# Splitting one pair of weight transfers into pieces of 15, 24 and 25 partitions

## The chip, the core and the metric

The kernel runs on one core of one Trainium2 chip. A core has a matrix engine (TensorE, PE in the profile), three engines for elementwise work (VectorE or DVE, ScalarE or ACT, GpSimd or POOL), a synchronising engine (SyncE, SP) and 16 DMA engines, which move data between the chip's main memory and the on-chip memory of 128 partitions. The metric is the time of one execution in microseconds (us), taken on the device; lower is better.

## What is computed

Linear attention with a feature map, then a layer that mixes channels for 64 Fourier modes along the sequence, then a residual with a rectified product. In the reference's own terms, cut short:

```python
# q, k, v: 8 batches x 8 heads x 576 x 64; phi(x) = exp(+-(x @ w_phi)), scaled
kv = einsum('bhsf,bhsd->bhfd', phi(k), v);  z = sum(phi(k), axis=2)
x  = (phi(q) @ kv) / (phi(q) @ z + 1e-6)            # to 8 x 576 x 512
X  = rfft(x, axis=1)[:, :64]                        # 64 modes
Yr = einsum('bmd,mde->bme', Xr, w_r) - einsum('bmd,mde->bme', Xi, w_i)
Yi = einsum('bmd,mde->bme', Xr, w_i) + einsum('bmd,mde->bme', Xi, w_r)
u  = x + irfft(Y, n=576)
out = u + maximum(u @ w_ch, 0)
```

`w_r` and `w_i` hold 64 matrices of 512 x 512 in 32-bit floats, 67 MB each. They are by far the largest inputs, and every element is used once per execution.

## The kernel before

**Stages.** The first stage walks over 32 steps of attention (two heads of one batch, or one head of two batches, in each) and computes feature maps, attention, and the forward Fourier transform of the result into `XT`. The mode products run beside it, as soon as the heads that they need are done. When the attention is finished, a loop over the remaining groups of modes goes on until all are summed (lines 852 to 903), and a last stage of 18 units makes the output: products with the inverse transform and with `w_ch`, a rectifier, sums, and stores (lines 905 to 927).

**Groups of weights.** The weights come in 32 groups, numbered k = 0 to 31 (lines 108 and 109). Group k has a pair (g, gi): a block of input channels and a set of modes. From k = 8 on, a group is 8 modes x 128 channels, for the real and for the imaginary weights: two tiles `wr` and `wi` of 128 partitions x 8 x 512. The 28th group is k = 27, with g = 3 and gi = 3. Its products (`mode_mm`, line 438) accumulate in PSUM over the real tile first and the imaginary tile second, and `mode_sum` adds them to what earlier groups left in `Yacc`.

**How a group is loaded.** `weights(k)` (line 156) makes a list of four issues: real weights for partitions 0 to 63 (y = 0), real for 64 to 127 (y = 1), then imaginary for the two halves. Each is one DMA from GpSimd's queue (line 169) with 64 partitions x 4 modes x 1024 elements, which reads 32-bit floats and writes bfloat16: 512 KB written. Within a partition, a run of 1024 elements is contiguous on both sides. In the last loop, `modes_of(k, 0)` (line 834) issues the groups up to k + 2 before it computes group k, so k = 27 is issued in the turn of k = 25. The tiles `wr` and `wi` have three buffers each (line 45), so a group may be loaded when the products of the group three before it are done.

**What orders the work.** The program's order is written out by hand (`manual_schedule`, lines 561 and 849); each engine runs its instructions in that order and waits on semaphores. The transfers from GpSimd's queue share eight semaphores in rotation: a transfer waits until the one eight places before it has landed, so at most eight are in flight. TensorE's first product of a tile waits for the transfers of that tile. In the last loop a turn holds, on TensorE, the real products of the group, a product with `w_ch` (`psW`, line 700), a transposition (`pt`, line 689), the imaginary products, the transposition of the sum (`ptY`, line 831), and every second turn a regrouping by batch (`psZY`, lines 726 and 732).

Of the kernel before, what the change touches and what calls it, by code (L numbers as in the profile page):

```python
# [26 lines left out]
def kernel(  # L27
# [11 lines left out]
    nc = tc.nc  # L39
# [116 lines left out]
    def weights(k):  # L156
        g, gi = groups[k]
        W[k] = wt = {}
        for ri, w in ((0, moe_w_r), (1, moe_w_i)):
            for y in range(2):  # L160
                def issue(ri=ri, w=w, y=y):
                    if y == 0 and k == 0:
                        wt[ri] = Yacc.rearrange("p a e -> p (a e)").bitcast(BF16).rearrange(
                            "p (r m e) -> p r m e", r=2, m=8)[:, ri]
                    elif y == 0:
                        wt[ri] = pw.tile([128, 8, DMODEL], BF16, name=f"w{'ri'[ri]}", tag=f"w{ri}")
                    t = wt[ri][64 * y:64 * y + 64]
                    if gi >= 0:
                        nc.gpsimd.dma_start(  # L169
                            t.rearrange("p (m i) e -> p m (i e)", i=2),  # L170
                            w[8 * gi + y:8 * gi + 8:2, g * 128:(g + 1) * 128, :].rearrange(
                                "m (p i) e -> p m (i e)", i=2))
                    else:
                        m0 = 16 * (-1 - gi) + 8 * y
                        nc.gpsimd.dma_start(
                            t, w[m0:m0 + 8, g * 64:(g + 1) * 64, :].rearrange("m p e -> p m e"))
                due.append((k, issue))
# [383 lines left out]
    with tc.manual_schedule():  # L561
# [22 lines left out]
        for n in range(N + 2):  # L584
# [54 lines left out]
            e = n - (N + 2 - N_EARLY)  # L639
# [209 lines left out]
    with tc.manual_schedule():  # L849
        flip_x()  # L850
        flip_x()
        for k in range(k_out, 31):
            gi = groups[k][1]
# [36 lines left out]
        rows = slice(96, 128)  # L890
# [14 lines left out]
        at_end, t, free = [], 0, 0  # L905
# [52 lines left out]
```

## Time and profile before

| what | value |
|---|---|
| median of 3 runs | 447.03 us (446.74 to 447.61) |
| the profiled execution's own time | 446.91 us |
| its span in the profile | 445.1 us |
| TensorE busy, of the span | 312.2 us (70%) |
| VectorE busy | 292.9 us (66%) |
| ScalarE busy | 271.7 us (61%) |
| GpSimd busy | 217.6 us (49%) |
| weights, real: transfers from line 169 and line 175, median time from issue to landing | 62 of 512 KB, 18.7 us |
| weights, imaginary | 62 of 512 KB, 18.6 us |

No computing engine is busy over 70% of the span, while in all but the last slices of the profile's overview the 16 DMA engines are busy 90% or more. A DMA engine's work is listed by queue: q0 holds the transfers that GpSimd issues, q1 those of SyncE and ScalarE, and q8 the blocks of instructions that an engine fetches as it goes through its program. The overview gives a mean over the 16 DMA engines; where they differ from each other has to be read from the end of a stage, where some run out of work before others.

### The profile page before, as it was taken

How to read it: one execution, taken by the hardware profiler on the slowest of the kernel's cores; microseconds unless marked ns; L12 is line 12 of the kernel's file. 1: busy time of each engine (PE TensorE's matmuls, PEld its weight loads, DVE VectorE, ACT ScalarE, POOL GpSimd, SP SyncE). 2: the span in 40 equal slices, each digit the busy share in tenths (PEclk: the TensorE clock that was granted, in tenths of full speed). 3: DMA queues.
4: the chain of work that ended last, by engine and by line, in shares of the span. 5: the costliest groups of instructions: out<-in, count | busy, mean ns of one | idle time of the engine just before them, and what ended most of it. 6: DMA issues, size and time to landing. Idle time of an engine off the chain costs nothing.

```text
span 445.1 us, 11874 instructions
## 1 busy us (share of the span) xinstructions
PE 312.2 (70%) x4997; PEld 202.9 (46%) x4997; DVE 292.9 (66%) x420; ACT 271.7 (61%) x570; POOL 217.6 (49%) x301
## 2 busy tenths in 40 slices
PE   1668587675966776765464667776898768777992
PEld 0456465564655654554342544433444434433440
DVE  4788889889788688878643886653232445264782
ACT  3766787886786886786652866662254445354761
POOL 6776448585457566556542654441142222100891
PEclk9999999989596599799966998887699898999997
DMA  8999999999999999999999999999999999991797
GB/s 191 248 225 218 221 226 219 230 219 218 229 222 222 223 231 221 225 231 222 231 212 222 222 222 211 211 211 211 211 206 212 210 211 211 210 201 32 253 354 278
DMA packets 60885, 97.76 MB, mean 220 GB/s; under 512 B 3888, under 2 KB 28784, under 8 KB 60832
## 3 DMA queue, kind: packets, MB, share of 16 engines
q0 software_dynamic: 51888, 76.69, 95.7%
q1 hardware_dynamic: 8784, 20.26, 13.2%
q8 instruction: 39, 0.64, 0.5%
q10 hardware_dynamic: 160, 0.07, 0.1%
q14 instruction: 14, 0.11, 0.1%
HBM read 163.64 MB, written 9.44 MB: 389 GB/s over the span
## 4 chain that ended last, share of the span: by engine, by line
DMA 38%; PE 24%; DVE 22%; ACT 8%; issue 4%; POOL 3%; DVEq 0%; SPq 0%; ACTq 0%; POOLq 0%
DMA wi<-in_moe_w_i_dram 22%; DVE mkq L248 8%; DMA k<-in_k_dram 8%; DMA wr<-in_moe_w_r_dram 5%; DVE nd L337 3%; DVE xs_all L351 3%; PE psY L438 3%; PE psWe L409 2%; ACT AA L255 2%; ACT AA L259 2%; PE psB L772 2%; PE ptr L199 2%; PE psB L779 2%; PE psA L793 2%; DMA kn<-in_k_dram 2%
## 5 line engine op out<-in xcount | busy, mean ns | idle before, releaser
L285 POOL TENSOR_TENSOR vaug<-vn,ee 128x576 bf16<-128x576 f32 x64 | 73.2, 1164 | 50.3 <-ACT ee L270 46.5
L255 ACT ACTIVATE AA<-psT 128x1024 bf16<-128x1024 f32 x64 | 62.0, 1021 | 23.9 <-PE psT L223 23.2
L169 POOL DMA_DIRECT2D wr<-in_moe_w_r_dram x48 | 29.7, 619 | 73.5 <-PE psY L438 24.8
L277 ACT ACTIVATE e<-mkq 64x4 f32<-64x4 f32 (+1 forms) x128 | 26.3, 206 | 58.8 <-DVE mkq L248 56.4
L259 ACT ACTIVATE AA<-psk 128x1024 bf16<-128x1024 f32 x64 | 61.3, 1008 | 0.0
L169 POOL DMA_DIRECT2D wi<-in_moe_w_i_dram x48 | 29.9, 625 | 44.8 <-DMA wi<-in_moe_w_i_dram 17.2
L248 DVE TENSOR_REDUCE mkq<-psq 128x8 f32<-128x1024 f32 x32 | 38.9, 1217 | 0.6 <-PE psq L214 0.4
L248 DVE TENSOR_REDUCE mkq<-psk 128x8 f32<-128x1024 f32 x32 | 38.7, 1210 | 0.7 <-PE psk L214 0.7
L438 PE MATMUL psY<-wi,XT 128*32 128x512 bf16 x192 | 17.7, 442 | 27.2 <-DMA wi<-in_moe_w_i_dram 27.2
L438 PEld LDWEIGHTS <-XT 128*32 128x32 bf16 x384 | 14.9, 172 | 45.6 <-DMA wi<-in_moe_w_i_dram 20.6
L702 ACT CAST xw<-psW 128x512 bf16<-128x512 f32 x34 | 19.9, 585 | 25.5 <-PE psW L700 25.0
L700 PE MATMUL psW<-wchb,sT 128*128 128x512 bf16 x136 | 34.0, 395 | 0.0
L692 DVE COPY sT<-pt 128x1024 bf16<-128x1024 bf16 x17 | 11.8, 692 | 33.7 <-PE pt L689 33.7
L330 DVE TENSOR_TENSOR tB<-psNB,e 128x650 f32<-128x650 f32 x32 | 26.6, 831 | 9.5 <-PE psNB L320 9.0
L205 DVE COPY kT<-ptr 128x640 bf16<-128x640 bf16 x32 | 15.7, 491 | 25.7 <-PE ptr L199 25.7
L320 PEld LDWEIGHTS <-AA 128*128 128x128 bf16 x640 | 28.4, 109 | 8.2 <-issue 7.8
L199 PE MATMUL ptr<-ident_b,k 128*128 128x128 bf16 x160 | 17.9, 257 | 19.4 <-DVE qT L205 15.9
L223 PE MATMUL psT<-qT,w 64*128 64x512 bf16 x64 | 15.2, 463 | 22.4 <-DVE mkq L248 22.2
L301 PE MATMUL kvz<-vaug,AA 64*128 64x65 bf16 x1152 | 28.5, 208 | 2.1 <-DVE Yacc L453 1.3
L351 DVE TENSOR_TENSOR xs_all<-nd,rden 128x640 bf16<-128x640 f32 x32 | 28.5, 892 | 1.1
L337 DVE TENSOR_TENSOR nd<-psNA,tB 128x650 f32<-128x650 f32 x32 | 26.7, 835 | 3.7 <-DVE tB L330 0.5
L301 PEld LDWEIGHTS <-AA 64*128 64x128 bf16 x1152 | 24.2, 105 | 6.4 <-issue 2.1
(141 smaller groups left out, 732.0 us busy)
## 6 DMA issues: line engine op xcount, KB each, us to landing
wr<-in_moe_w_r_dram POOLq DMA_DIRECT2D x62, 512.0 KB, 18.7
wi<-in_moe_w_i_dram POOLq DMA_DIRECT2D x62, 512.0 KB, 18.6
out_dram<-of SPq DMA_DIRECT2D x14, 512.0 KB, 3.9
vn<-in_v_dram SPq DMA_DIRECT2D x24, 288.0 KB, 6.0
q<-in_q_dram POOLq DMA_DIRECT2D x12, 288.0 KB, 16.7
k<-in_k_dram POOLq DMA_DIRECT2D x12, 288.0 KB, 16.8
vn<-in_v_dram SPq DMA_DIRECT2D x16, 144.0 KB, 6.7
Yacc<-in_moe_w_r_dram POOLq DMA_DIRECT2D x2, 512.0 KB, 8.8
```

What stands on the lines that cost most here:

```text
L169: nc.gpsimd.dma_start(t.rearrange("p (m i) e -> p m (i e)", i=2), w[8 * gi + y:8 * gi + 8:2, g * 128:(g + 1) * 128, :].rearrange("m (p i) ...
L199: nc.tensor.transpose(ptr[:, c, :], tb[:, 2 * c:2 * c + 2, :].rearrange("p j d -> p (j d)"), ident_b,)
L248: nc.vector.tensor_reduce(out=o, in_=i, axis=AX.X, op=ALU.max, apply_absolute_value=True)
L255: nc.scalar.activation(AA[:, 0, ab, 0:1024].rearrange("f (x j p) -> f j x p", j=2, p=64), st["psT"].rearrange("f j (x p) -> f j x p", p=64 ...
L259: nc.scalar.activation(AA[:, 1, ab, 0:1024].rearrange("p (c j f) -> p j c f", c=4, j=2), st["psk"], ACT.Exp, scale=sc)
L285: nc.gpsimd.tensor_tensor(out=vaug[:, ab, :, 0:64], in0=st["v"], in1=ee[:, ab, :].unsqueeze(2).to_broadcast([128, 9, D_]), op=ALU.mult,)
L301: nc.tensor.matmul(kvz[:, hh, ab * 65:(ab + 1) * 65], lhsT=AA[r, 1, ab, 128 * j:128 * j + 128], rhs=vaug[r, ab, j, :], start=(j == 0), sto ...
L320: nc.tensor.matmul(p[:, hh, 65 * c:65 * c + 65], lhsT=AA[:, 0, ab, x:x + 128], rhs=kvzF[:, hh, ab * 65:(ab + 1) * 65], start=True, stop=True,)
L337: nc.vector.tensor_tensor(out=nd, in0=st["psNA"], in1=st["tB"], op=ALU.add)
L351: nc.vector.tensor_tensor(out=xo, in0=nd[:, :, :, 0:64], in1=rden.to_broadcast([128, 2, NCH, 64]), op=ALU.mult,)
L438: nc.tensor.matmul(psY[32 * j:32 * j + 32, :], lhsT=XT[:, 16 + 32 * ri:48 + 32 * ri, 32 * i + 4 * gi + j], rhs=wt[ri][:, 2 * j + i, :], st ...
L700: nc.tensor.matmul(ps, lhsT=sT[:, x, dc, :], rhs=wchb[:, dc, :], start=(dc == 0), stop=(dc == 3))
```

## The change

For group k = 27, and there for the real weights alone, each of the two transfers of 64 partitions is issued as three: partitions 0 to 14, 15 to 38 and 39 to 63 of the half, that is 15, 24 and 25 partitions. The bytes, the source rows and the destination are the same. All other groups, and the imaginary weights of this one, keep their transfers of 64 partitions.

```diff
                     if gi >= 0:
-                        nc.gpsimd.dma_start(
-                            t.rearrange("p (m i) e -> p m (i e)", i=2),
-                            w[8 * gi + y:8 * gi + 8:2, g * 128:(g + 1) * 128, :].rearrange(
-                                "m (p i) e -> p m (i e)", i=2))
+                        dst = t.rearrange("p (m i) e -> p m (i e)", i=2)
+                        rows = w[8 * gi + y:8 * gi + 8:2, g * 128:(g + 1) * 128, :].rearrange(
+                            "m (p i) e -> p m (i e)", i=2)
+                        cuts = (0, 15, 39, 64) if k == 27 and ri == 0 else (0, 64)
+                        for p0, p1 in zip(cuts, cuts[1:]):
+                            nc.gpsimd.dma_start(dst[p0:p1], rows[p0:p1])
```

## The prediction

> **What bounds the kernel now.** I read the chain of waits first, cut to the time after 305 us. Columns: start in us, length in us, what the end waited for.
>
> ```profile
> 325.73 0.60 POOL wi L169
> 326.33 18.80 DMA wi<-in_moe_w_i_dram
> ...
> 345.41 19.72 DMA wi<-in_moe_w_i_dram
> ...
> 365.41 19.60 DMA wi<-in_moe_w_i_dram
> ...
> 385.30 19.60 DMA wi<-in_moe_w_i_dram
> 404.90 0.04 issue
> 404.94 0.69 PE psY L438 x8
> 405.63 0.54 PE psA L787 x2
> ```
>
> From 326 to 404.9 us the end waits for nothing but weight transfers. What follows the last landing, up to the end of the run, is a chain of its own: 446.91 - 404.90 = 42.0 us (446.91 is the profiled execution, with a span of 445.1). A change before 405 us counts as far as it moves the last landing.
>
> Next, GpSimd's queue in order of time (start, length, instruction, idle time before it and its releaser), around group 27, which the diff splits: the two wr rows are what it replaces.
>
> ```profile
> 338.20 0.61 POOL L169 DMA_DIRECT2D wr<-in_moe_w_r_dram  x1 [2.13 <-DMA wr<-in_moe_w_r_dram]
> 340.44 0.61 POOL L169 DMA_DIRECT2D wr<-in_moe_w_r_dram  x1 [1.62 <-DMA wr<-in_moe_w_r_dram]
> 343.22 0.61 POOL L169 DMA_DIRECT2D wi<-in_moe_w_i_dram  x1 [2.18 <-PE psW L700]
> 345.41 0.61 POOL L169 DMA_DIRECT2D wi<-in_moe_w_i_dram  x1 [1.57 <-DMA wi<-in_moe_w_i_dram]
> ```
>
> An issue takes 0.61 us, then GpSimd idles 1.6 to 2.2 us until an older transfer has landed. In the built program each transfer waits for the semaphore of the eighth transfer before it, so eight are in flight. Later rows of the view have the first wi of a group at 343.22 and at 383.06 us, four groups or 16 transfers apart: 39.84 / 16 = **2.49 us per transfer**. That agrees with 512 KB at 211 GB/s (2.485 us), so the transfers run back to back.
>
> Third, busy time in short stretches up to the last landing. The last two columns are the mean busy share of the 16 DMA engines (about 1.12 when all are busy, since packets overlap) and GB/s.
>
> ```profile
> 398.00:399.00 1.00, 0.76 (x10) 0.64 (x10) 0.30 (x2) 0.12 (x1) 0.00 (x0) 1.00 1.14 215
> 399.00:400.00 1.00, 1.00 (x7) 0.41 (x5) 0.57 (x1) 0.26 (x1) 0.00 (x0) 1.00 0.79 147
> 400.50:401.00 0.50, 0.50 (x9) 0.27 (x8) 0.00 (x0) 0.39 (x1) 0.00 (x0) 1.00 0.64 119
> 402.50:403.00 0.50, 0.50 (x4) 0.22 (x3) 0.00 (x0) 0.28 (x1) 0.00 (x0) 1.00 0.56 106
> 403.50:404.00 0.50, 0.00 (x0) 0.00 (x0) 0.00 (x0) 0.14 (x1) 0.00 (x0) 1.00 0.31 57
> 404.00:404.50 0.50, 0.00 (x0) 0.00 (x0) 0.00 (x0) 0.00 (x0) 0.00 (x0) 1.00 0.18 33
> ```
>
> The engines do not finish together. Soon after 399 us about half have run out of work (0.64 / 1.12 = 57% are left at 400.5 us, 50% at 402.5), and the rest need until 403 to 404.5 us. The trace's landing signs say the same: a transfer gives sixteen, and those of the last one come in two groups of eight, from 399.43 to 401.48 and from 403.58 to 404.90 us. This spread of 5.4 us is the same for every transfer after 330 us, so both groups run at one pace and one is behind. The queue rows suggest what put it behind:
>
> ```profile
> q0 software_dynamic: 51888, 76.69, 95.7%
> q8 instruction: 39, 0.64, 0.5%
> ```
>
> Blocks of instructions used 0.5% of 16 x 445.1 us = 35.6 us of DMA engine time, 39 packets of 0.91 us. In the packet records their lengths repeat every eight packets, as if eight engines took them in turn: 35.6 / 8 = 4.5 us each, about the gap between the groups. So the late eight would be those that also fetch instructions. Full levelling could win: engine time left after 399.0 us, over all stretches, is 3.02 us by shares, / 1.12 = 2.70, so a level end at 401.7 in place of 404.5 us, **2.8 us at most**.
>
> **The change, part by part.**
>
> *Bytes and their shares.* Nothing is removed: 128 partitions of group 27's real weights move as before, in runs of the same length. A transfer of 64 partitions gives an engine 64 / 16 = 4, so one partition costs 2.49 / 4 = **0.62 us** on its engine, and an engine that gets p of the 128 in place of 8 moves by (p - 8) x 0.62. All later transfers have even shares, so a shift stays to the last landing. No row shows how 15, 24 or 25 partitions are dealt. The bounds are -2.8 us (levelled) and, if a piece of 25 stays with a single engine in both halves, (50 - 8) x 0.62 = +26 us; with 64 or 128 partitions, the only transfers of weights, q and k here, the shares are equal. I stay by these rows: equal shares on as many engines as divide the piece, the next piece going on where the last one stopped. That is 15 engines with 1, 12 with 2, 5 with 5: 32 runs, twice round the ring, so the second half repeats the first. Per half, 11 engines get 1 + 2 = 3, four get 1 + 5 = 6, one gets 2 + 5 = 7 (33 + 24 + 7 = 64). Over both halves eleven have 6 in place of 8 (-1.24 us), four 12 (+2.49), one 14 (+3.73). The Trainium skill, DMA: Bandwidth & Descriptors, section "Why a DMA increments its semaphore by 16 and not by 1", states such a rule: the largest count up to 16 that divides the slowest dimension, on consecutive engines from a round-robin cursor; no run here shows it yet, and its exception is the first rival.
>
> *On whom the surplus falls.* No row numbers the engines. I assume that both the pieces and the instruction blocks are dealt from the first engine on: then the surplus falls on the last five and the late group is the first eight. The late eight move by -1.24; the surplus engines, of the early group, end at most at 401.48 + 2.49 = 403.97 or near 399.5 + 3.73 = 403.2, against 404.90 - 1.24 = 403.66. So the gain is 0.93 to 1.24 us; I take 1.24, as only one of the early eight is as late as 401.48.
>
> *Four more transfers.* Each engine posts four more landing signs; the packet records show 22 ns for one: +0.09 us. By the Trainium skill, same page, "Anatomy of one DMA", a transfer from GpSimd costs some 2.0 us beside its bytes, which would make +8 us if it were paid in turn. The pace of 2.49 us is bytes alone, so here it is hidden.
>
> *GpSimd's queue.* Four more issues, 4 x 0.61 = 2.44 us, lie in its idle time. But the pieces take six places of the eight in flight: they are issued one per landing, from 338.2 to about 350.5 us, and group 27's two wi behind them at 352.9 and 355.4 in place of 343.2 and 345.4. The cover shrinks by four transfers, from 19.6 us to about 10. The late engines begin the pieces at 355.1 us and have 6 x 0.62 + 2.49 = 6.2 us of work before they need the second wi, issued at 355.4; a 64 KB transfer from GpSimd lands 2.0 us after issue (list of DMA issues), so 4.2 us of cover are left: cost 0. Without this cover it would be up to the 2.0 us. The early engines, 5.4 us ahead, may idle 1 to 1.5 us there, which costs nothing while they stay 4 us ahead. Next are group 28's transfers, which wait for the pieces' semaphores and so go out within 3 us of each other.
>
> *TensorE.* Its first wr product of group 27 waits for six semaphores in place of two; behind it stand psW, pt and the wi products. The last piece lands near 359 us, before TensorE gets there at 360.7, so no cost. TensorE must take up the earlier landings (timeline of PE):
>
> ```profile
> 365.17 0.69 PE L438 MATMUL psY<-wi,XT 128*32 128x512 bf16 x8 [1.53 <-DMA wi<-in_moe_w_i_dram]
> ...
> 404.94 0.69 PE L438 MATMUL psY<-wi,XT 128*32 128x512 bf16 x8 [1.49 <-DMA wi<-in_moe_w_i_dram]
> ```
>
> It is idle 1.53 and 1.49 us ahead of them, more than is won, so the gain passes through; 1.49 is its ceiling.
>
> **Sum:** -1.24 + 0.09 = -1.15; 446.91 - 1.15 = **445.8 us**. The median of the runs shown is 447.03, 0.12 above the profiled one; the same step from it gives 445.9.
>
> **Rivals.**
> 1. *Slower: dealt by rounding up from the first engine.* 15 as 1 on 15 engines, 24 as 2 on 12, 25 as 2 on 12 and 1 on one: twelve engines get 5 of 64, the others 3, 1, 1, 0. At most four engines are relieved and at least four late ones get 10 in place of 8. It decides as soon as one of those near 404.9 is among the twelve: +1.24 + 0.09 = +1.33, 448.2 us. For it: nothing in the rows but that it also gives 4 each for 64. The Trainium skill, in the section named first, reports as an exception that some copies from GpSimd were dealt so (100 partitions on engines 0 to 14); no run here shows it.
> 2. *Slower: equal runs, but the surplus meets late engines.* A late engine with 12 in place of 8 ends 2.49 later: +2.58, 449.5 us; with 14, up to +3.8, 450.7. For it: half of all engines are late. Against: they look like one block of eight. The Trainium skill, same page, "Latency and other measured facts", calls engines 7 and 15 usually the slow ones, and engine 15 would have the 14; this trace shows eight late ones, not two.
> 3. *The shares stay even.* Then only +0.09, 447.0 us.
>
> **Chances.** Forecast 0.56, first rival 0.18, second 0.14, third 0.12. A measurement of this kernel tells about 0.2% (0.9 us) from no change, so faster 0.56, same 0.12, slower 0.32. The likeliest case alone is 445.4 (TensorE's ceiling) to 446.1 (gain of 0.84). The range goes from 445.2 (the ceiling, and the runs' own scatter of some 0.3 us below their median) to 448.6, over the first rival; the second is left out, and with it the +26 us of a piece on one engine, which no row comes near.
>
> **What would show it.** Right: the last landing near 403.7 us; the late half's stretch shorter by 1.2 us with the early half's end spread to 402 to 403; GpSimd's six issues some 2.5 us apart; TensorE idle only 0.3 us ahead of the last wi products; 42.0 us after the landing unchanged. Rival 1: two groups still, the last landing near 406.2. Rival 2: one to five engines alone at 407 or later. Wrong altogether: a stretch after 350 us in which the late engines idle, or an issue of a piece that takes several us.

## The result, and the profile after

The change made the kernel slower: median 450.09 us (449.5 to 450.88, 4 runs) against 446.88 us before, ratio 1.007 with a 95% interval of 1.0058 to 1.0083, some 3.2 us. The forecast was 445.8 us, and its range ended at 448.6; the second rival (equal runs, surplus on late engines) had 449.5. The profiled execution took 449.50 us with a span of 447.7 us.

The chain of waits of the changed kernel, cut to its last part (start, length, what the end waited for):

```profile
355.67 12.27 DMA wi<-in_moe_w_i_dram
...
368.23 19.59 DMA wi<-in_moe_w_i_dram
...
388.10 19.58 DMA wi<-in_moe_w_i_dram
407.68 0.04 issue
407.72 0.67 PE psY L440 x7
```

It is still weight transfers to the last landing, at 407.68 us in place of 404.90: **+2.78 us**. What follows is 449.50 - 407.68 = 41.8 us long, 42.0 before. So all of the loss lies ahead of the last landing. (Of the 3.2 us between the medians, the profiled pair shows 2.6; the changed kernel's profiled execution was its fastest.)

GpSimd's queue around group 27 (start, length, instruction, idle time before it and its releaser):

```profile
338.44 0.60 POOL L174 DMA_DIRECT2D wr<-in_moe_w_r_dram  x1 [2.22 <-PE ptY L833]
340.58 0.60 POOL L174 DMA_DIRECT2D wr<-in_moe_w_r_dram  x1 [1.54 <-DMA wr<-in_moe_w_r_dram]
343.07 0.68 POOL L174 DMA_DIRECT2D wr<-in_moe_w_r_dram  x1 [1.89 <-DMA wi<-in_moe_w_i_dram]
345.54 0.54 POOL L174 DMA_DIRECT2D wr<-in_moe_w_r_dram  x1 [1.80 <-DMA wi<-in_moe_w_i_dram]
348.06 0.57 POOL L174 DMA_DIRECT2D wr<-in_moe_w_r_dram  x1 [1.97 <-DMA wr<-in_moe_w_r_dram]
350.52 0.68 POOL L174 DMA_DIRECT2D wr<-in_moe_w_r_dram  x1 [1.88 <-DMA wr<-in_moe_w_r_dram]
353.75 0.64 POOL L174 DMA_DIRECT2D wi<-in_moe_w_i_dram  x1 [2.55 <-PE psY L440]
355.67 0.62 POOL L174 DMA_DIRECT2D wi<-in_moe_w_i_dram  x1 [1.29 <-DMA wi<-in_moe_w_i_dram]
356.77 0.61 POOL L174 DMA_DIRECT2D wr<-in_moe_w_r_dram  x1 [0.47 <-DMA wr<-in_moe_w_r_dram]
```

The six pieces go out one per landing, 2.1 to 2.5 us apart, the two wi behind them at 353.8 and 355.7 us, and then group 28 quickly. The issue times are within a microsecond of those worked out. No issue takes longer than 0.68 us.

Busy time by stretch (the last two columns are the mean busy share of the DMA engines, 1.12 when all are busy, and GB/s), first around the pieces, then up to the last landing:

```profile
345.00:350.00 5.00, 3.38 (x44) 1.72 (x48) 1.11 (x2) 0.00 (x0) 1.12 (x2) 0.65 1.12 210
350.00:355.00 5.00, 4.95 (x60) 2.20 (x54) 2.43 (x2) 2.59 (x3) 1.32 (x2) 0.67 1.00 177
...
401.00:402.00 1.00, 0.48 (x6) 0.36 (x7) 0.42 (x1) 0.00 (x0) 0.00 (x0) 1.00 0.71 131
403.00:404.00 1.00, 1.00 (x5) 0.39 (x4) 0.25 (x1) 0.57 (x1) 0.00 (x0) 1.00 0.40 76
405.00:406.00 1.00, 1.00 (x6) 0.49 (x5) 0.00 (x0) 0.12 (x1) 0.00 (x0) 1.00 0.29 55
406.00:407.00 1.00, 1.00 (x6) 0.29 (x3) 0.00 (x0) 0.72 (x2) 0.00 (x0) 1.00 0.22 41
407.00:408.00 1.00, 0.42 (x6) 0.37 (x8) 0.00 (x0) 0.33 (x1) 0.00 (x0) 1.00 0.04 6
```

Two things are new. From 350 to 355 us the engines move 177 GB/s in place of 210, at a busy share of 1.00 in place of 1.12: some of them stand still for a part of the time. And the end has a third step: from 405 to 407 us the share is 0.29 to 0.22, that is 0.29 / 1.12 x 16 = 4.1 engines. **Four engines run on alone.** The trace's sixteen landing signs of the last transfer, one for each DMA engine, in us, show the same (the bar stands where the wide gap is):

```
before: 399.43 399.47 399.51 399.51 399.71 399.91 400.51 401.48 | 403.58 403.59 403.60 404.05 404.17 404.78 404.85 404.90
after:  401.38 401.39 401.44 401.48 401.58 401.62 401.92 402.19 402.34 403.26 404.11 404.31 | 406.61 407.34 407.44 407.68
```

TensorE in order of time, at group 27's two products:

```profile
363.64 0.68 PE L440 MATMUL psY<-wr,XT 128*32 128x512 bf16 x8 [1.68 <-DMA wr<-in_moe_w_r_dram]
...
367.99 0.67 PE L440 MATMUL psY<-wi,XT 128*32 128x512 bf16 x8 [1.39 <-DMA wi<-in_moe_w_i_dram]
```

The wr product now waits 1.68 us for the pieces, where it had been covered; the last piece landed at 363.5 us, not near 359.

Not all of the 2.78 us comes from the pieces. The landing that frees GpSimd at 335 us, before any piece is issued, is at 335.18 us before and at 335.32 with the change. From there to the last landing it is 69.72 us before and 72.36 with the change: **+2.64 us**. The landing at 335 us is used as a common start below, too; it holds to 0.1 or 0.2 us, as the engine that is last there need not be the last at the end.

### The profile page after: what moved, and what is told of

Same layout as the page of the kernel before. It is cut to its first block, busy times and chain, and to the rows that moved or that the text cites. A ratio compares the mean times of both kernels' runs of the same rounds, so it can differ in the third digit from the quotient of the medians.

```text
span 447.7 us, 11864 instructions
## 1 busy us (share of the span) xinstructions
PE 309.8 (69%) x4979; PEld 202.2 (45%) x4997; DVE 294.6 (66%) x420; ACT 271.8 (61%) x570; POOL 218.8 (49%) x305
## 4 chain that ended last, share of the span: by engine, by line
DMA 49%; DVE 19%; PE 16%; ACT 7%; issue 4%; POOL 3%; DVEq 0%; ACTq 0%; POOLq 0%
DMA wi<-in_moe_w_i_dram 26%; DMA wr<-in_moe_w_r_dram 15%; DVE mkq L250 7%; DMA Yacc<-in_moe_w_i_dram 4%; DMA k<-in_k_dram 4%; DVE nd L339 3%; ACT AA L257 3%; DVE xs_all L353 3%; PE psA L795 2%; PE psY L440 2%; PE psB L774 2%; PE psB L781 2%; DVE tB L332 2%; PE psNB L322 1%; ACT AA L261 1%
## 5 line engine op out<-in xcount | busy, mean ns | idle before, releaser
L174 POOL DMA_DIRECT2D wr<-in_moe_w_r_dram x52 | 32.1, 618 | 80.4 <-PE psY L440 23.1
L702 PE MATMUL psW<-wchb,sT 128*128 128x512 bf16 x126 | 33.0, 395 | 0.8 <-issue 0.3
L353 DVE TENSOR_TENSOR xs_all<-nd,rden 128x640 bf16<-128x640 f32 x32 | 29.9, 936 | 1.1
L225 PE MATMUL psT<-qT,w 64*128 64x512 bf16 x64 | 14.1, 430 | 22.8 <-DVE mkq L250 22.6
```

The source lines that it names most:

```text
L174: nc.gpsimd.dma_start(dst[p0:p1], rows[p0:p1])
L353: nc.vector.tensor_tensor(out=xo, in0=nd[:, :, :, 0:64], in1=rden.to_broadcast([128, 2, NCH, 64]), op=ALU.mult,)
L702: nc.tensor.matmul(ps, lhsT=sT[:, x, dc, :], rhs=wchb[:, dc, :], start=(dc == 0), stop=(dc == 3))
```

## The experiments

Every time is a median, and every ratio is to the kernel before, run beside it on the same chip. "Ring" means the 16 DMA engines in the order in which uneven pieces are dealt to them; its engine 0 is the one where the change's first piece begins, and no run tells which of the chip's engines that is.

### Six even pieces, and two other orders of the same pieces

**Six even pieces.**

```diff
-cuts = (0, 15, 39, 64) if k == 27 and ri == 0 else (0, 64)
+cuts = (0, 16, 32, 64) if k == 27 and ri == 0 else (0, 64)
```

> Six pieces as in the change, but of 16, 16 and 32 partitions, which share evenly over 16 engines. Theory S (unequal shares: four of the late DMA engines got 12 partitions in place of 8, so +2.5 us): the shares are even again, only four more transfers remain: 446.9 to 447.3 us, last landing near 405 us. Rival Q (six transfers in place of two: GpSimd's queue, the places among the eight in flight, the pieces' own cost): as the change, 449.5 to 450.1 us, last landing near 407.7.

447.26 us, ratio 1.0007 (0.9992 to 1.0022). So six transfers in place of two explain little of the loss. The windows of its profile show what the pieces do cost, in the share of the DMA engines near the end:

```profile
401.00:402.00 1.00, 1.00 (x6) 0.49 (x5) 0.48 (x1) 0.35 (x1) 0.00 (x0) 1.00 0.82 154
403.00:404.00 1.00, 1.00 (x9) 0.50 (x6) 0.00 (x0) 0.10 (x1) 0.00 (x0) 1.00 0.46 86
404.00:405.00 1.00, 1.00 (x7) 0.39 (x5) 0.00 (x0) 0.62 (x2) 0.00 (x0) 1.00 0.27 49
```

The early half ends only after 401.7 us (its landing signs: 401.72 to 402.20; before: 399.43 to 401.48), since it stood still behind the small pieces (a busy share of 1.08 from 350 to 360 us, 1.13 before). The last landing is at 405.42, 0.5 us later than before; but the landing at 335 us is at 335.58 here, 0.4 us late before any piece is issued. From there to the last landing it is 69.84 us, 0.12 more than before. Against the even pieces the change has 72.36 - 69.84 = +2.52 us, which is four partitions at 0.62.

**The same pieces in another order.** `(0, 25, 49, 64)` gives 25, 24, 15, and `(0, 15, 40, 64)` gives 15, 25, 24.

> The change's pieces in the order 25, 24, 15. Theory S with runs that go on round the ring from where the last piece stopped: the change put the surplus on the last five engines of a turn, four of them late; this order puts it on the first five (14 partitions on the first, 12 on the next four), which follow the late block: late engines get 6 in place of 8, last landing 403.7 to 404.7 us (1.24 earlier, less up to 0.9 for what the small pieces cost), time 445.8 to 446.8. Rival Q and a dealing in which each piece begins at the same engine: the order changes nothing, 449.5 to 450.1 us.

> The change's pieces in the order 15, 25, 24. Theory S: the piece of 25 now falls on the last engine of the turn and the first four of the next, so the surplus is 14 on one early engine and 12 on four early ones: 445.8 to 446.8 us, as for the order 25, 24, 15. Rival Q: 449.5 to 450.1 us.

446.66 us for the first, ratio 0.9992 (0.9981 to 1.0003); 446.38 us for the second, ratio 0.9980 (0.9964 to 0.9995). Sizes, number of transfers, bytes and waits are those of the change, which has 1.007: **the order alone decides.** A dealing in which each piece begins at the same engine cannot do that. (The first of the two is not clear of the kernel before, and its expected last landing of 403.7 to 404.7 us did not come: in its profiled execution, at 447.42 us slower than its median, it is at 405.49, with two engines alone at 405.10 and 405.49. Why this order wins less is open.) The windows of the order 15, 25, 24:

```profile
401.00:402.00 1.00, 0.85 (x10) 0.37 (x10) 0.00 (x0) 0.60 (x2) 0.00 (x0) 1.00 0.98 182
402.00:403.00 1.00, 1.00 (x6) 0.49 (x5) 0.00 (x0) 0.12 (x1) 0.00 (x0) 1.00 0.70 131
403.00:404.00 1.00, 1.00 (x6) 0.29 (x3) 0.00 (x0) 0.72 (x2) 0.00 (x0) 1.00 0.30 55
404.00:405.00 1.00, 0.88 (x10) 0.48 (x10) 0.01 (x1) 0.33 (x1) 0.00 (x0) 1.00 0.00 0
```

Now the engines end within 2.6 us of each other (landing signs 401.61 to 404.22), no step is left at the end, and TensorE takes up the last weights at 404.26 us. Against the even pieces the last landing moved from 405.42 to 404.22, -1.20 us, from the same landing at 335 us (335.58 and 335.56): the two partitions of relief at 0.62 us each.

**Half a dose**, the change in its first half alone (`... and ri == 0 and y == 0`):

> Only the first half (partitions 0 to 63) is cut into 15, 24 and 25; the second half stays one transfer. Theory S: four late engines have 10 in place of 8, half the dose: +1.24 us and up to 0.4 for the pieces: 448.1 to 448.6 us, last landing 406.1 to 406.6. Rival Q: two more transfers in place of four; if their cost is in the queue's places, about half as well, so this run tells the size of the step, not the cause.

448.11 us, ratio 1.0024 (1.0012 to 1.0036), last landing at 405.92 us: about the half (the time is at the lower edge of what was named, the landing 0.2 us below it). From the landing at 335 us (334.80 here) it is 71.12 us, +1.40 over before: half of the 2.49, and some 0.2 for the pieces.

### What sets the place where a piece begins

**Small transfers ahead.** One of 5 partitions early in the kernel and one of 11 behind the last weights; and the same without the second:

```diff
+    spare = [const.tile([128, 128], BF16, name=f"spare{i}") for i in range(2)]
...
         issue_weights(2)
+        nc.gpsimd.dma_start(spare[0][0:5], w_phi[0:5])
...
+                        if k == 31 and ri == 1 and y == 1:
+                            nc.gpsimd.dma_start(spare[1][0:11], w_phi[0:11])
```

> The change's own pieces in its own order 15, 24, 25, but a small transfer of 5 partitions from GpSimd (into a spare tile that nothing reads) goes out early in the kernel, and one of 11 partitions after the last weights, so that the five and eleven make one turn of 16. Theory S with a place on the ring that is carried from piece to piece: the surplus moves on by five engines and falls on early ones only; as the orders 15, 25, 24 and 25, 24, 15: 445.8 to 446.8 us, faster than before by 0.2 to 1.0. If the order of the sizes within a half is what counts, and not the place on the ring: as the change, 449.5 to 450.5 us.

> The same without the last small transfer of 11 partitions: each execution of this kernel then moves the place on the ring by 5. If the place is carried over from one execution to the next: the executions of this one kernel scatter between about 446 (surplus on early engines, 4 places of 16) and 451 us (14 partitions on a late one), more than 3 us apart. If it begins anew with each execution: all near 446 us, within the 2 us or so in which runs of one kernel lie.

449.79 us, ratio 1.0056 (1.0035 to 1.0076), and 449.53 us, 1.0049 (1.0030 to 1.0068): both as the change, and the second no more scattered than others (448.56 to 451.04). Theory S had expected the first fast and the second scattered, or near 446 us throughout; neither came. Next, the small transfer right ahead of the pieces, with the change's order, and one of 11 with the good order:

```diff
+                        if k == 27 and ri == 0 and y == 0:
+                            nc.gpsimd.dma_start(spare[0:5], w_phi[0:5])
                         for p0, p1 in zip(cuts, cuts[1:]):
```

> The change as it is, with the small transfer of 5 partitions issued right ahead of the first piece, with no transfer of 64 or 128 partitions between. Theory S1 (the place on the ring is carried from one uneven piece to the next, but a transfer that uses all 16 engines sets it back): the surplus moves on by five engines to early ones: 445.8 to 447.0 us. Theory S2 (where a piece begins depends on its own rows in the tile, not on what came before it): as the change, 449.5 to 450.3 us.

> The good order 15, 25, 24, with a small transfer of 11 partitions right ahead of the first piece. S1: the surplus moves from early engines onto five late ones, one of them with 14 partitions: +2.5 to +4.2 us, 449.5 to 451.2. S2: as the order 15, 25, 24 alone, 446.2 to 446.8 us.

449.79 us, ratio 1.0054 (1.0034 to 1.0075), and 446.81 us, 0.9997 (0.9982 to 1.0013). With the change's order four engines are alone at the end as before (407.01 to 408.11 us), and with the good order none is later than 405.91. The small transfers did not move the place; S1 falls for them. But with the good order no gain is left: from 355 to 360 us the engines move 159 GB/s, without the small transfer 194.

**A large uneven pair ahead**, from another tile:

```diff
+                        if k == 26 and ri == 1 and y == 1:
+                            cuts = (0, 9, 64)
```

> The change as it is, and the transfer right ahead of its first piece (second half of group 26's imaginary weights) cut into 9 and 55 partitions: nine engines with 1, then eleven with 5, 20 runs, so the place would move on by 4. Where the place is carried from one uneven piece to the next, whatever tile it belongs to (C1): the change's surplus falls on engines 15 and 0 to 3 of the ring, all early, and the late four (11 to 14) have 5 + 6 of 192 where 12 is even (-0.6 us); 446 to 447.8 us. Where the place begins anew with each tile or half (C2): the late four have 5 + 12 = 17, +3.1 us and the pieces' own cost: 450.2 to 451.2 us.

448.53 us, ratio 1.0027 (1.0014 to 1.0040), between the two. The landing signs settle it: the last transfer has one engine at 406.64 us, alone, and no group of four; the next is at 404.91. With the place moved on by 4, engine 3 of the ring has 6 + 14 = 20 where 12 is even, +4.97 us. Early engines end from 401.7 us on with pieces in the queue (the even pieces), and 401.7 + 5.0 = 406.7. The expectation for C1 had left out this engine and the early engines' idling. The size is fitted behind the result, and roughly: by the same working the three early engines with 18 would end at 405.4, yet none but the one is later than 404.91. What decides is that one engine is alone and not four. Had each tile begun anew, the late four would be at the end together, 3.1 us behind. So large uneven pieces do carry the place on, also from tile to tile. Why the small ones do not is **open**.

### The dose, and the ring

**More of the good order.** Pieces in one and a half and in two doses:

```diff
+                        if k == 27 and ri == 0:
+                            cuts = (0, 15, 40, 64)
+                        if k == 27 and ri == 1 and y == 0:
+                            cuts = (0, 25, 40, 64)
```

> One and a half doses: real weights of group 27 as 15, 25, 24 in both halves, and the first half of its imaginary weights as 25, 15, 24. Theory S: late engines lose 3 of 192 partitions' eights in place of 2 (-1.86 us in place of -1.24), two more small transfers cost up to 0.2; the five or six early engines with the surplus get up to 7 more than even (+4.4 us), and end near 404. So 0.2 to 0.6 below the order 15, 25, 24: 445.6 to 446.4 us. If the early engines' stay idle behind the small pieces is what limits: no gain on it, 446.4 or above.

447.18 us, ratio 0.9998 (0.9986 to 1.0010): no gain is left. Its landing signs spread over 2.3 us only, but end at 404.96: the engines are level, and all end later than with the order 15, 25, 24 (404.22, from the same landing at 335 us). The early ones lost more time behind nine small pieces: the first sign comes at 402.66, 73.51 us after the first sign of the transfer that lands at 335 us; with the six pieces of that order it is 71.23.

> Two doses on the same engines: real and imaginary weights of group 27 both as 15, 25, 24. Theory S: late engines -2.5 us, but one early engine gets 28 in place of 16 (+7.5) and four get 24 (+5.0); these become the last, at 404.5 to 408 us, alone: 447 to 450 us, slower than before although it is twice what made it faster; in the landing signs one to five engines at the end. If relief of the late engines alone counted: 445.2 us.

449.88 us, ratio 1.0051 (1.0035 to 1.0068). The windows of its profile:

```profile
404.00:405.00 1.00, 1.00 (x6) 0.39 (x4) 0.26 (x1) 0.57 (x1) 0.00 (x0) 1.00 0.36 68
405.00:406.00 1.00, 1.00 (x11) 0.37 (x10) 0.00 (x0) 0.60 (x2) 0.00 (x0) 1.00 0.25 47
406.00:407.00 1.00, 1.00 (x6) 0.49 (x5) 0.00 (x0) 0.13 (x1) 0.00 (x0) 1.00 0.08 14
407.00:408.00 1.00, 1.00 (x6) 0.29 (x3) 0.00 (x0) 0.72 (x2) 0.00 (x0) 1.00 0.06 12
408.00:409.00 1.00, 0.40 (x5) 0.27 (x8) 0.00 (x0) 0.32 (x1) 0.00 (x0) 1.00 0.02 4
```

From 407 to 408 us the share is 0.06, which is 0.06 / 1.12 x 16 = 0.9: one engine alone. Its landing signs are eleven up to 403.67, four from 405.76 to 406.44, and one at 408.68: the four engines with 12 + 12 and the one with 14 + 14, as dealt on paper, and the same pieces that had won 0.2% lose 0.5%.

**49 and 15** in one half (`(0, 49, 64)`), and **15 and 49** (`(0, 15, 64)`):

> One half of group 27's real weights cut in two, 49 and 15. S1: 49 goes as 7 on each of 7 engines, all early ones (the ring's first seven after the late block), 15 as 1 on the other nine and on six of these. All late engines get 1 in place of 4 (-1.86 us), the seven early ones 7 or 8 (+1.9 to +2.5): last landing 403.1 to 404.0, time 445.5 to 446.4 us, 0.6 to 1.4 faster than before with one more transfer in place of four. S2 leaves open where each piece begins: if both began at the first of the 16, some late engine would have 8: +2.5 us or no gain.

> The same half cut as 15 and 49. S1: 15 goes to all but the sixteenth engine, the run of seven begins with that one: 7 on it, 8 on the next six, all early: 445.5 to 446.6 us. S2: as for 49, 15 or worse.

448.95 us, ratio 1.0041 (1.0027 to 1.0055), and 448.23 us, 1.0029 (1.0014 to 1.0043). The signs behind the piece of 49 tell whom the run of seven meets, as a partition is 0.62 us: in the first kernel five early engines and two late ones (at the end 406.23 and 407.29, the next at 403.99), in the second, where the run begins one engine earlier, six early and one late (407.18, the next at 403.90). So engines 15 and 0 to 4 of the ring are early, 5 and 6 late; with 11 to 14, the late four of the change, that leaves 7 to 10, two of each kind. The late eight are not one block, as the expectations and the forecast had them.

**20 and 44**, then 44 and 20, made with this ring:

```diff
+                        if k == 27 and y == 0:
+                            cuts = (0, 44, 64) if ri else (0, 20, 64)
```

> One half of group 27's real weights as 20 and 44, one half of its imaginary weights as 44 and 20, a whole transfer between. With the ring as read from the runs with 49 and 15 (0 to 4 and 15 early, 5, 6 and 11 to 14 late) and both cuts beginning at engine 0: 20 is 2 on 0 to 9, 44 is 4 on 10 to 15 and 0 to 4; 44 is 4 on 0 to 10, 20 is 2 on 11 to 15 and 0 to 4. Engines 0 to 4 get 12 in place of 8, engine 10 gets 8, all others 6: late engines -1.24 us, with two more transfers in place of four. 445.7 to 446.4 us, level with or up to 0.5 below the order 15, 25, 24. If the second cut begins elsewhere (the first moved the place by 21, so 5 on): late engines 5 to 9 get 2 + 6, even, and 10 to 14 get 4 + 4: no gain, 447.0 to 447.5 us.

447.36 us, ratio 1.0007 (0.9995 to 1.0019): what was named for a second cut that begins where the first one ended, although a whole transfer of 64 lay between. Dealt so, every engine has 8 in all, and the landing signs agree: two groups of eight, 399.93 to 401.39 and 403.71 to 405.45 us. Had both cuts begun at engine 0, five early engines with 12 would have left the first group.

**The order 15, 25, 24 once more:**

> The order 15, 25, 24 once more, on this chip beside the two others and the kernel before: 0.1 to 0.35% below the kernel before, as the first time (0.2%, interval 0.05 to 0.36).

445.88 us, ratio 0.9974 (0.9964 to 0.9984). This version beats the kernel before both times, by 0.20% and 0.26%, and the change by 0.9%. From the landing at 335 us to the last it takes 68.66 us both times, 1.06 less than before.

## Why the prediction was wrong

**The step that failed is "on whom the surplus falls".** It assumed that pieces and instruction blocks are both dealt "from the first engine on: then the surplus falls on the last five and the late group is the first eight". In fact four of the five surplus engines are late ones. They got 12 in place of 8, and the term of -1.24 us became +2.49. With the 0.12 us that six even pieces cost by themselves that makes +2.61; from the landing at 335 us on, +2.64 were measured, and the remaining 0.14 of the 2.78 were there before the pieces. Nothing in the page numbered the engines, and half of all engines are late, so a block in the right place was the optimistic reading; 0.56 was too high a chance.

**Bytes and shares: right.** The equal runs of 15 x 1, 12 x 2 and 5 x 5 can be counted, in the page's row on packets of the changed kernel:

```profile
DMA packets 61461, 97.76 MB, mean 218 GB/s; under 512 B 4464, under 2 KB 29360, under 8 KB 61408
```

Before there were 3888 packets under 512 B, so 576 are new; four more transfers with 16 signs each are 64, and 512 are left, 256 for each half. They are 4-byte packets in the trace. If an engine without a share gets as many of them as a sharing engine has packets of data (four per partition), equal runs give 1 x 4 + 4 x 8 + 11 x 20 = 256; rounding up (15, 12, 13 engines) would give 1 x 4 + 4 x 8 + 3 x 8 = 60. The same count holds for other sizes: 49 and 15 have 272 more packets than before (16 signs, 9 x 28 and 4), 20 and 44 with 44 and 20 have 288 (32 signs and twice 6 x 8 + 5 x 16). That and the order experiments put the first rival out. The Trainium skill, DMA: Bandwidth & Descriptors, section "Why a DMA increments its semaphore by 16 and not by 1", has this rule, the largest dividing count on consecutive engines from a cursor that goes round; the large pieces here agree with it, and its exception by rounding up does not apply to them. By the same rule the small transfers of 5 and 11 partitions would move the cursor, too; here they left it where it was (1.0056, 1.0054 and 0.9997).

**The price of a partition: right.** 0.62 us: the change against six even pieces (+2.52 for +2.49), the order 15, 25, 24 against them (-1.20 for -1.24) and half a dose (+1.40 for +1.24 and the pieces) fit it.

**Four more transfers: right in size.** +0.09 us was the term; the even pieces show 0.12 us from the landing at 335 us to the last. Their median is 0.2 us higher (ratio 1.0007, interval -0.08 to +0.22%), so in time it is not resolved.

**GpSimd's queue: right on issue times** (350.5, 352.9 and 355.4 us forecast; 350.5, 353.8 and 355.7 measured), **and on idle early engines, not on their price.** "1 to 1.5 us there, which costs nothing" has the size too small and the price right only while they have no surplus to work off. With even pieces the foremost engine loses some 3 us (from the first sign of the transfer that lands at 335 us to the first of the last one it is 72.57 us, 69.60 before), and with a surplus that comes on top, as in the two doses and behind 9 and 55.

**TensorE: the cover was lost.** "The last piece lands near 359 us" held for engines with six partitions; the piece ends with its slowest engine, at 363.5 us.

**The second rival was the outcome**: a late engine with 12 in place of 8, 449.5 us (that the profiled execution took just this is in part luck, as the median is 450.09); its sign in the profile, a few engines alone at 407 us or later, is what the windows show. That the late eight are those that fetch instructions was argued from the sums of time, and no run was made to test it, but the landing signs before the change bear it out. Nine blocks of instructions start between 274 and 392 us. After each of them one sign of the late eight stands 1.0 to 1.1 us later than before it, for all transfers that follow, and none of the early eight moves by more than some 0.5 us, apart from one stop of all early ones near 326 us. In the changed kernel the blocks at 376.74 and 394.24 us each put back one of the four engines that end last, by 1.0 to 1.1 us: engines with the surplus are engines that fetch.

## What to carry to other kernels

When the end waits for a stream of transfers on all DMA engines, look at how the engines finish: a stretch at half the busy share means that some are behind, and that a re-deal of the bytes could win up to the way from the last engine's end to a level end (here 2.8 us, of which some 1 us was got). Unequal shares are a tool with a sign: the same six pieces gained 0.2% or lost 0.7% by their order, so find out which engines are late, on that kernel, before choosing, and try each order. Each extra transfer also takes one of the places in flight, and here the engines that were ahead lost up to 3 us behind small pieces.

## What the runs showed of the hardware that was not expected

- A piece that does not go to all 16 engines puts one 4-byte packet on each of the others for each packet of data that a sharing engine has: 256 for 15, 24 and 25 partitions. The kernel with half a dose has 4177 packets under 512 B: 289 more than before, 32 signs and 257, one over.
- The place where a piece begins goes on from large piece to large piece, over tiles (9 and 55) and over a whole transfer between (20 and 44), but not from transfers of 5 or 11 partitions with one packet for each partition. All kernels with a sum of runs that is no multiple of 16 kept to one level over their executions (49 and 15: 447.72 to 450.04 us in 12), so nothing shows it carried from one execution to the next.
- The late engines lie at 5, 6 and 11 to 14 of the ring, with two more among 7 to 10, and are not neighbours all eight. A block of instructions (16 KB, some 0.9 us on its engine) puts one of them back by 1.0 to 1.1 us, and between 330 us and the last landing that delay stayed.
